# mLSTM cell and leaky-ReLU feed-forward: another order of rows for w_in and x, and values loaded by one request

## The chip, the cores and the metric

The kernel runs on one core of a Trainium2 chip. The metric is the time of one execution on the device in microseconds (us); lower is better. Engines are named as in the profile: PE is TensorE (PEld its weight loads), DVE is VectorE, ACT is ScalarE, POOL is GpSimd, SP is SyncE, whose queue (SPq) issues nearly all DMAs of this kernel.

## What is computed

An mLSTM cell over 4 batches, 8 heads, 768 tokens and head dimension 40 gives `y`, and a feed-forward block follows (3072 tokens, model width 320, inner width 2048). Inputs q, k, v, the gates i, f, o, and the weights `w_in` (320 x 2048) and `w_out` (2048 x 320), which come as 64-bit floats.

```python
for t in range(S):
    m_new = np.maximum(f[:, :, t] + m, i[:, :, t])
    f_stab, i_stab = np.exp(f[:, :, t] + m - m_new), np.exp(i[:, :, t] - m_new)
    m = m_new
    C = f_stab * C + i_stab * outer(v_t, k_t)
    n = f_stab * n + i_stab * k_t
    y[:, :, t] = sigmoid(o_t) * (C @ q_t) / np.maximum(np.abs(n @ q_t), 1.0)
x = y.transpose(0, 2, 1, 3).reshape(B * S, H * D)      # 3072 x 320
h = x @ w_in
out = np.maximum(0.01 * h, h) @ w_out
```

## The kernel before

**Steps.** Time is cut into 6 chunks of 128 tokens. A step `s` is one chunk of one batch, so there are 24 steps, `c, b = divmod(s, 4)`. Each chunk gives 512 tokens (4 batches x 128), one group of the feed-forward block. While group `c - 1` runs through the feed-forward block on TensorE, the cells of chunk `c` are computed between its pieces: `ff_units` makes a list of some 30 pieces per group, `cell_units` the list of cell parts, and the main loop (L1043 to L1103) calls a piece and then those cell parts whose place in a list written by hand (`place` for chunk 1, `pairs` later) has come. PE, DVE, ACT and POOL run in the order in which the program issues; so does SP's queue, where an instruction that waits holds up all behind it.

**Three kinds of steps.** Chunk 0 (steps 0 to 3) is written out in `first_chunk`. Steps 4 to 7 (chunk 1) use `u_parts` and `u_plain`. Steps 8 to 23 use `u_parts` and `u_mix`. `ahead(s)` prepares a step some pieces before it is needed: `prep_qs` (L487) or `prep_kq` (L505, L511), loads for step `s + 2`, `state_next` (L592, the old state times its decay, on POOL), `prep_vu` (L478, keys times gates, on POOL) and in some places `prep_mask` (L450, the mask added to the decay tile `w`, on POOL). `feed(s)` loads k (L356) and v (L359) and then `spread(s)` loads the decay rows into `w` (L413). `u_parts` multiplies scores (L614) and the new state (L619, which reads the values from the state tile `S` and the scaled keys of L478), then L624 and L596 on DVE.

**Values.** From chunk 1 on, the values of a step stand in the tile `S` (`S_v[n]`, n = s % 4) in two halves of tokens and two halves of 20 of the head dimension with a gap between. Four requests per step put them there directly from DRAM.

**x and w_in.** The feed-forward block needs x transposed, `xT`: the 320 features lie as 5 slots of 64 on 64 partitions, twice (on partitions 0 to 63 and 64 to 127), because two matmuls of 64 rows work side by side for two different columns of `w_in` (L759, `w_row`). The slots of the two halves stand in different orders (`SLOTS`), and a slot holds 64 neighbouring features. In chunks 0 and 1, `gate` (L650, L654) or `u_plain` (L676, L681) makes x with tokens on partitions, and `u_x` transposes it on PE (L742, L743) and copies it to `xT` by five copies on ACT (L745 to L749). From chunk 2 on, `u_mix` makes x transposed in blocks of 32 on DVE (L702, L706, L709 on POOL, L713), stores it to a DRAM tile `x_dr` by four requests (L716), and `gather_x` reads it back by four (L730) into `xT`, a tile with one buffer, after the last L759 of the group before.

**Weights.** `load_weights(n)` loads a slab of `w_in` by ten requests (L229) or one of `w_out` by one (L234); `narrow_weights` turns 64-bit floats into 32-bit ones on ACT (L247) and DVE (L249 to L263), in small pieces that the main loop issues between units of chunk 1.

**The end of a group.** `fast_units` multiplies by `w_out` in 14 products (L835) whose results are combined by DVE (L862, L887, L892), ACT and POOL (L868, L876, L882). The PSUM banks of `ph` and `po` are four, used in turn, so that the first L759 of the next group needs banks that L887 has read.

Of the kernel before, what the change touches and what calls it, by code (L numbers as in the profile page):

```python
# [9 lines left out]
F32 = mybir.dt.float32  # L10
# [8 lines left out]
def kernel(  # L19
# [26 lines left out]
    nc = tc.nc  # L46
# [19 lines left out]
    KF = Dm // P  # L66
    KR = Dm - KF * P
    KC = Dm // DP
    SLOTS = ([0, 2, 4, 1, 3], [1, 3, 0, 2, 4])
    assert NB * P == S and NF * P == FF and NF % 4 == 0 and D <= DP and H == 2 * PR and BH <= P  # L70
    assert KR == DP and KC == 5 and KC * DP == Dm and GT * 4 <= 2048

# [101 lines left out]
        at = (2 * slot + e) * P  # L174
        return w_in[DP * r : DP * (r + 1), n, at : at + P]

    def run_of(r, at):

        ks = SLOTS[r][at:]
        return ks[0], next((i for i in range(1, len(ks)) if ks[i] != ks[i - 1] + 2), len(ks))  # L180

    HW = 2 * Dm
    wide = moe_w_in.dtype == U64
    raws = {}
# [19 lines left out]
    def load_weights(n):  # L204

        m = n - QN
        if n < QN:
            dst = w_in[:, n, :]
        else:
            dst = w_out[:, 2 * m : 2 * m + 2, :].rearrange("p a d -> p (a d)")  # L210
        to = dst
        if wide:
            if n < 2:
                at = NF * GT - 2 * WC * (n + 1)
                raw = acts_l[:, at : at + 2 * WC].bitcast(U64)
            elif n < QN:
                raw = raw_t[:, WC * (n - 2) : WC * (n - 1)]
            elif m < 2:
                raw = w_out[:].rearrange("p f d -> p (f d)")[:, (2 + m) * WC : (3 + m) * WC].bitcast(U64)
            else:  # L220
                at = (4, 0, 1, 2, 3, 4)[m - 2] * HW
                raw = raw_t[:, at : at + HW]
            raws[n] = (raw, dst)
            to = raw
        if n < QN:
            src = moe_w_in[:, n * QC : (n + 1) * QC].rearrange("(k p) (r c) -> r p k c", p=DP, r=2)
            for slot in range(KC):
                for r in range(2):
                    nc.sync.dma_start(  # L229
                        to[DP * r : DP * (r + 1), 2 * P * slot : 2 * P * (slot + 1)], src[r, :, SLOTS[r][slot], :],  # L230
                    )
        else:
            rows = moe_w_out[2 * m * P : 2 * (m + 1) * P, :]
            nc.sync.dma_start(to.rearrange("p (a d) -> p a d", d=Dm), rows.rearrange("(a p) d -> p a d", p=P))  # L234
# [29 lines left out]


    a_dr = dr.tile([NB, 2, 2, BH, SL], F32, name="a_dr")
    x_dr = dr.tile([NS, Dm, P], F32, name="x_dr")
    gT, gL = {}, {}
    m0s = {}
    bus = {}  # L270
# [73 lines left out]
    def load(s):  # L344
        c, b = divmod(s, B)
        rows = ts(c, P)
        d = st.setdefault(s, {})
        n = s % NL
        d.update(k=kn[:, n], q=qn[:, n])
        if c == 0:  # L350
            d["va"] = S_t[n][:, 1]
            parts = [(d["k"][:, :, :D], k), (d["q"][:, :, :D], q), (d["va"][:, :, :D], v)]
            for dst, src in parts:
                nc.sync.dma_start(dst, src[b, :, rows, :].rearrange("h p d -> p h d"))
            return
        nc.sync.dma_start(d["k"][:, :, :D], k[b, :, rows, :].rearrange("h p d -> p h d"))  # L356
        for u in range(2):
            for i in range(2):
                nc.sync.dma_start(  # L359
                    S_v[n][ts(u, SL), u, :, i, :DB],  # L360
                    v[b, :, c * P + u * SL : c * P + (u + 1) * SL, DB * i : DB * (i + 1)].rearrange("h p d -> p h d"),
                )

    def load_o(s):
        c, b = divmod(s, B)
# [6 lines left out]
    def natural(s, i):  # L372

        t = rb_t[s % NR][:, i]
        return t[:, : H * D].rearrange("p (h d) -> p h d", d=D)
# [30 lines left out]
    def spread(s):  # L406

        c, b = divmod(s, B)
        d = st[s]
        w = wk.tile([P, H, P], F32, name="w", bufs=NL)  # L410
        d["w"] = w[:].rearrange("p h t -> p (h t)")[:, : H * SL].rearrange("p (h t) -> p h t", t=SL)
        for u in range(2):
            nc.sync.dma_start(d["w"][ts(u, SL)], a_dr[c, 0, u, b * H : (b + 1) * H, :].partition_broadcast(SL))  # L413

# [230 lines left out]
    def gate(s):  # L645

        d = st[s]
        d["x"] = wk.tile([P, Dm], F32, name="x")
        x3 = d["x"][:].rearrange("p (h d) -> p h d", d=D)
        nc.vector.scalar_tensor_tensor(  # L650
            x3, in0=d["o"].rearrange("p (h d) -> p h d", d=D), scalar=1.0, in1=d["pa"][:, :, :D],
            op0=ALU.add, op1=ALU.mult,
        )
        nc.gpsimd.tensor_tensor(x3, x3, d["den"][:].unsqueeze(2).to_broadcast([P, H, D]), op=ALU.mult)  # L654

    def u_plain(s):

        c, b = divmod(s, B)
        d = st[s]
        prep_o(s)  # L660
        hN = psc.tile([P, H, 2, V1], F32, name="hN", tag="c")
        m = mixed(s)
        for h in range(H):
            for u in range(2):
                nc.tensor.matmul(
                    hN[ts(u, SL), h].rearrange("p k d -> p (k d)"), lhsT=m[:, u, h, :], rhs=S_v[s % NL][:, u, h, :, :V1],
                    start=True, stop=True,
                )
        state_next(s, 1)
        den = wk.tile([P, H], F32, name="den")  # L670
        denominators(den[:], hN[:, :, 0, DB])
        if b < 2:
            d["x"] = wk.tile([P, Dm], F32, name="x")[:]
        else:
            d["x"] = wk.tile([P, H, D1], F32, name="hn")[:].rearrange("p h d -> p (h d)")[:, :Dm]
        nc.vector.scalar_tensor_tensor(  # L676
            d["x"].rearrange("p (n d) -> p n d", d=DB), in0=natural(s, 2).rearrange("p h (k d) -> p (h k) d", d=DB), scalar=1.0,
            in1=hN[:].rearrange("p h k d -> p (h k) d")[:, :, :DB], op0=ALU.add, op1=ALU.mult,
        )
        x3 = d["x"].rearrange("p (h d) -> p h d", d=D)  # L680
        nc.gpsimd.tensor_tensor(x3, x3, den[:].unsqueeze(2).to_broadcast([P, H, D]), op=ALU.mult)  # L681
        state_add(s, 1)

    def u_mix(s):
# [26 lines left out]
            state_add(s, 1)  # L711
        xq = wk.tile([P, PR * P], F32, name="x")
        nc.vector.transpose(in_blocks(xq[:]), xb[:].rearrange("p (j n) d -> p j n d", n=TB))  # L713
        to = x_dr[s].rearrange("(j n i) t -> n i j t", n=4, i=DB)
        for n in range(4):
            nc.sync.dma_start(to[n], xq[QW * n : QW * n + DB].rearrange("p (j t) -> p j t", t=P))  # L716
        del st[s]

    def gather_x(s):

        c, b = divmod(s, B)
        if ("xT", c) not in st:
            st["xT", c] = wk.tile([P, KC, GT], F32, name="xT", bufs=1)
        xT = st["xT", c]
        src = x_dr[s].rearrange("(k p) t -> p k t", p=DP)
        for r in range(2):
            at = 0
            while at < KC:
                k0, n = run_of(r, at)
                nc.sync.dma_start(xT[DP * r : DP * (r + 1), at : at + n, ts(b, P)], src[:, k0 : k0 + 2 * n - 1 : 2, :])  # L730
                at += n

    def u_x(s):

        c, b = divmod(s, B)
        d = st[s]
        if b == 0:
            st["xT", c] = wk.tile([P, KC, GT], F32, name="xT", bufs=1)
        xT = st["xT", c]
        xt = psc.tile([P, KF + 1, P], F32, name="xt", tag="c")  # L740
        for kk in range(KF):
            nc.tensor.transpose(xt[:, kk, :], d["x"][:, ts(kk, P)], ident[:])  # L742
        nc.tensor.transpose(xt[:KR, KF, :], d["x"][:, KF * P :], ident[:])  # L743
        tok = ts(b, P)
        nc.scalar.copy(xT[:, :KF, tok], xt[:, :KF, :])  # L745
        nc.scalar.copy(xT[:DP, KF + 1 :, tok], xt[DP:, :KF, :])
        nc.scalar.copy(xT[DP:, KF : 2 * KF, tok], xt[:DP, :KF, :])
        nc.scalar.copy(xT[:DP, KF, tok], xt[:DP, KF, :])
        nc.scalar.copy(xT[DP:, 2 * KF, tok], xt[:DP, KF, :])  # L749
        del st[s]  # L750


    def ff_units(g):
        xT = st["xT", g]

        def rows(j, ph, cols, slots):
            for slot in slots:
                for r in range(2):
                    nc.tensor.matmul(  # L759
                        ph[r][:, cols], lhsT=w_row(r, slot, j), rhs=xT[DP * r : DP * (r + 1), slot, cols],  # L760
                        start=(slot == 0), stop=(slot == KC - 1),
                    )

# [17 lines left out]

        def half(j, h):
            ph = [psf.tile([P, GT], F32, name=f"ph{r}", tag="mm") for r in range(2)]
            cols = ts(h, GT // 2)
            rows(j, ph, cols, range(KC))
            relu(j, ph, cols)

# [131 lines left out]
    def ahead(s):  # L919

        if s < NS:
# [9 lines left out]
            if s + NR < NS:  # L931
                load_late(s + NR, 0)
                load_late(s + NR, 1)
                if s + NR >= 2 * B:
                    spread_q(s + NR)
            state_next(s, 0)
            prep_vu(s)
            if s + 1 <= 2 * B:
                prep_mask(s + 1)
# [195 lines left out]
```

## Time and profile before

| | |
|---|---|
| time, median of 3 runs | 510.27 us (510.13 to 510.55) |
| span of the profiled execution, first to last instruction | 508.0 us |
| median less this span | 2.27 us |
| mean granted TensorE clock | 0.983 |
| requests of v in chunks 1 to 5 (L359) | 80 of 40 KB |
| stores of x (L716), gathers (L730) | 64 of 40 KB, 32 of 96 KB and 32 of 64 KB |
| DMA packets | 165290, of these under 512 B 128816 |
| DMA engines' share of the span, queue of SP | 52.2% |

The profiled execution has no time of its own beside its span; what lies around the span is taken as the difference to the median. Times inside the profile count from the first instruction. A line such as L759 is a line of the kernel before. Rows of groups give busy time and mean duration of one instruction, then the idle time of its engine just before. Matmul ends are modelled, and each f32 matmul appears as two records.

### The profile page before, as it was taken

The numbers are of one execution on the slowest core, as the hardware profiler recorded it, in microseconds if no ns is written. First come the engines' busy times: TensorE is split into PE (matmuls) and PEld (weight loads), VectorE is DVE, ScalarE is ACT, GpSimd is POOL, SyncE is SP. The second block draws the span as 40 slices with busy tenths as digits, with TensorE's granted clock in tenths as the row PEclk, the third lists the DMA queues.
The fourth block names the chain that finished last, engine by engine and source line by source line (L and its number), as shares of the span: only waits on it lengthen the run. The fifth ranks groups of instructions, "written<-read, shape, count | busy, mean of one in ns | idle before, by whom it ended". The sixth has DMA issues, their size and how long they took to land.

```text
span 508.0 us, 12526 instructions
## 1 busy us (share of the span) xinstructions
PE 492.0 (97%) x4981; PEld 366.6 (72%) x4981; DVE 308.1 (61%) x515; ACT 171.5 (34%) x478; POOL 137.7 (27%) x175
## 2 busy tenths in 40 slices
PE   8878999999999999999999999999899999999997
PEld 7766878767655489955589855599755599744797
DVE  4779898899954778635765826764825664101321
ACT  3664864652722510323411323311213411022210
POOL 4243443360402404413104614014612003000020
PEclk9877999999999999999999999999999999999999
DMA  9977687888765551565663566564466212200001
GB/s 116 146 204 154 149 219 185 168 152 175 155 145 87 131 124 46 133 130 144 147 132 92 115 137 170 137 141 97 109 135 177 68 53 62 69 1 1 1 1 52
DMA packets 165290, 59.21 MB, mean 117 GB/s; under 512 B 128816, under 2 KB 156016, under 8 KB 165232
## 3 DMA queue, kind: packets, MB, share of 16 engines
q1 hardware_dynamic: 164848, 58.28, 52.2%
q8 instruction: 39, 0.64, 0.5%
q14 instruction: 19, 0.16, 0.1%
q10 hardware_dynamic: 384, 0.13, 0.1%
HBM read 51.68 MB, written 6.70 MB: 115 GB/s over the span
## 4 chain that ended last, share of the span: by engine, by line
PE 79%; DVE 9%; DMA 3%; ACT 3%; POOL 2%; issue 2%; SPq 2%; ACTq 0%; POOLq 0%; DVEq 0%
PE ph L759 36%; PE po L835 26%; PE po L794 6%; PE pT L695 3%; PE sd L614 3%; SPq L359 1%; PE sd L619 1%; DMA S<-in_v_dram 1%; ACT kqT L540 1%; PE tkq L548 1%; DVE raw L261 1%; DMA rb<-in_q_dram 1%; DMA w<-a_dr 1%; PE pa L641 1%; DVE qn L511 1%
## 5 line engine op out<-in xcount | busy, mean ns | idle before, releaser
L759 PE MATMUL ph<-xT,w_in 64*128 64x512 f32 (+1 forms) x1120 | 216.2, 538 | 2.4 <-DVE y L887 1.4
L759 PEld LDWEIGHTS ph<-xT,w_in 64*128 64x128 f32 x1120 | 108.6, 189 | 95.1 <-issue 86.3
L767 ACT ACTIVATE acts<-ph 128x512 f32<-128x512 f32 (+1 forms) x112 | 53.9, 533 | 179.0 <-PE ph L759 178.9
L835 PEld LDWEIGHTS po<-w_out,acts 128*128 128x128 f32 x640 | 87.3, 190 | 3.8 <-issue 3.8
L835 PE MATMUL po<-w_out,acts 128*128 128x160 f32 x640 | 89.1, 300 | 0.0
L450 POOL TENSOR_TENSOR w<-w,i 128x512 f32<-128x512 f32 x20 | 26.9, 1345 | 117.3 <-DMA w<-a_dr 117.2
L624 DVE TENSOR_TENSOR qn<-w,sd 64x512 f32<-64x512 f32 x40 | 27.4, 684 | 40.2 <-PE sd L619 20.5
L458 ACT ACTIVATE w<-w,gT 128x64 f32<-128x64 f32 (+1 forms) x192 | 50.8, 348 | 2.7 <-POOL w L450 1.7
L592 POOL TENSOR_TENSOR S<-S,f 40x336 f32<-40x336 f32 x36 | 32.0, 889 | 67.3 <-PE pT L695 36.3
L835 PE MATMUL po<-raw,acts 128*128 128x160 f32 x320 | 45.5, 300 | 0.0
L835 PEld LDWEIGHTS po<-raw,acts 128*128 128x128 f32 x320 | 43.9, 190 | 0.3
L794 PE MATMUL po<-w_out,acts 128*128 128x320 f32 x128 | 36.5, 436 | 0.0
L702 DVE STREAM_TRANSPOSE hb<-pT 128x512 f32<-128x512 f32 x16 | 11.5, 717 | 31.0 <-PE pT L695 30.8
L794 PEld LDWEIGHTS po<-w_out,acts 128*128 128x128 f32 x128 | 23.6, 190 | 9.3 <-issue 0.3
L511 DVE TENSOR_TENSOR qn<-kqT,ea 64x512 f32<-64x512 f32 x32 | 28.4, 888 | 1.0
L709 POOL TENSOR_TENSOR xb<-xb,den 128x320 f32<-128x320 f32 x16 | 11.7, 729 | 56.8 <-DVE xb L706 56.6
L596 DVE TENSOR_TENSOR S<-S,sd 40x336 f32<-40x336 f32 x36 | 18.1, 503 | 12.1 <-POOL S L592 11.2
L614 PEld LDWEIGHTS sd<-kqT 40*64 40x64 f32 x640 | 19.9, 135 | 6.1 <-issue 6.1
L822 DVE TENSOR_TENSOR raw<-acts 128x1024 f32<-128x1024 f32 x10 | 11.8, 1222 | 18.3 <-ACT acts L767 18.2
L713 DVE STREAM_TRANSPOSE x<-xb 128x512 f32<-128x512 f32 x16 | 18.2, 1140 | 7.6 <-POOL xb L709 7.6
L835 PE MATMUL po<-raw 128*128 128x160 f32 x160 | 22.5, 299 | 0.0
L835 PEld LDWEIGHTS po<-raw 128*128 128x128 f32 x160 | 22.0, 190 | 0.0
(151 smaller groups left out, 551.8 us busy)
## 6 DMA issues: line engine op xcount, KB each, us to landing
w<-a_dr SPq DMA_DIRECT2D x40, 128.0 KB
rb<-in_k_dram SPq DMA_DIRECT2D x64, 80.0 KB
rb<-in_q_dram SPq DMA_DIRECT2D x64, 80.0 KB
rb<-in_o_gate_dram SPq DMA_DIRECT2D x64, 80.0 KB
ea<-a_dr SPq DMA_DIRECT2D x32, 128.0 KB
kn<-in_k_dram SPq DMA_DIRECT2D x24, 160.0 KB
raw<-in_moe_w_out_dram SPq DMA_DIRECT2D x6, 640.0 KB
S<-in_v_dram SPq DMA_DIRECT2D x80, 40.0 KB
```

The lines of the kernel that those rows point to most:

```text
L450: nc.gpsimd.tensor_tensor(w, w, cm2.unsqueeze(1).to_broadcast([P, H, SL]), op=ALU.add)
L458: yield nc.scalar.activation(w[:, h, :], w[:, h, :], AF.Exp, bias=gT[c][:, 0, bh : bh + 1], scale=1.0)
L511: nc.vector.tensor_tensor(mixed(s)[rows, 1 - r], d["kqT"][rows, 1].rearrange("p (h t) -> p h t", t=SL), d["ea"][rows], op=ALU.mult,)
L592: nc.gpsimd.tensor_tensor(new, old, g, op=ALU.mult)
L596: nc.vector.tensor_tensor(new, new, st[s]["dC", u], op=ALU.add)
L614: nc.tensor.matmul(bank[1 - u][toks, h, :], lhsT=kqT[rows, 0, ts(h, SL)], rhs=kqT[rows, 1, ts(h, SL)], start=True, stop=True,)
L624: nc.vector.tensor_tensor(mixed(s)[toks, u], w[toks], bank[1 - u][toks], op=ALU.mult)
L713: nc.vector.transpose(in_blocks(xq[:]), xb[:].rearrange("p (j n) d -> p j n d", n=TB))
L759: nc.tensor.matmul(ph[r][:, cols], lhsT=w_row(r, slot, j), rhs=xT[DP * r : DP * (r + 1), slot, cols], start=(slot == 0), stop=(slot == KC ...
L767: nc.scalar.activation(acts[:, f, cols], ph[r][:, cols], AF.Prelu, alpha=0.01)
L794: nc.tensor.matmul(po[n][:], lhsT=acts[:, f, ts(n, P)], rhs=w_out[:, f, :], start=(f == 0), stop=(f == NF - 1),)
L835: nc.tensor.matmul(bank[:], lhsT=left[:, f, :], rhs=right[:, f, :], start=f == 0, stop=f == KH - 1)
```

## The change

Feature `5 p + k` now stands on partition `p` in slot `k`, for both halves alike, in `w_in` and in `xT`. `u_mix` stores the whole 128-partition tile with its padding rows in one request; `gather_x` reads 64 partitions of 2560 contiguous bytes in one request for each half. `xT` is laid out by batch first, so that L759 reads it in runs of 128 columns. In chunks 0 and 1 x is written in the new order by the DVE instruction of `gate` and `u_plain`, multiplied in that order by POOL (`scale_x`), and `u_x` needs four copies in place of five. The values of a step from chunk 1 on are loaded by one request into an unused part of the tile `w` (which is now allocated in `load`), and `place_v`, called in `ahead` between `state_next` and `prep_vu`, copies them into `S` by two POOL instructions.

```diff
-    SLOTS = ([0, 2, 4, 1, 3], [1, 3, 0, 2, 4])
...
-            src = moe_w_in[:, n * QC : (n + 1) * QC].rearrange("(k p) (r c) -> r p k c", p=DP, r=2)
+            src = moe_w_in[:, n * QC : (n + 1) * QC].rearrange("(p k) (r c) -> r p k c", p=DP, r=2)
...
-                        to[DP * r : DP * (r + 1), 2 * P * slot : 2 * P * (slot + 1)], src[r, :, SLOTS[r][slot], :],
+                        to[DP * r : DP * (r + 1), 2 * P * slot : 2 * P * (slot + 1)], src[r, :, slot, :],
...
-        for u in range(2):
-            for i in range(2):
-                nc.sync.dma_start(
-                    S_v[n][ts(u, SL), u, :, i, :DB],
-                    v[b, :, c * P + u * SL : c * P + (u + 1) * SL, DB * i : DB * (i + 1)].rearrange("h p d -> p h d"),
-                )
+        w = wk.tile([P, H, P], F32, name="w", bufs=NL)
+        flat = w[:].rearrange("p h t -> p (h t)")
+        d["w"] = flat[:, : H * SL].rearrange("p (h t) -> p h t", t=SL)
+        d["vn"] = flat[:, H * SL : H * (SL + D)].rearrange("p (h d) -> p h d", d=D)
+        nc.sync.dma_start(d["vn"], v[b, :, rows, :].rearrange("h p d -> p h d"))
+
+    def place_v(s):
+        for u in range(2):
+            toks = ts(u, SL)
+            nc.gpsimd.tensor_copy(
+                S_v[s % NL][toks, u, :, :, :DB], st[s]["vn"][toks].rearrange("p h (k d) -> p h k d", d=DB),
+            )
...
+    def x_by(x, m):
+        return x[:].rearrange("p (k m a) -> p m a k", k=KC, m=m)
+
+    def scale_x(x, den):
+        x4 = x[:].rearrange("p (k h a) -> p k h a", k=KC, h=H)
+        by = den[:].unsqueeze(1).unsqueeze(3).to_broadcast([P, KC, H, DP // H])
+        nc.gpsimd.tensor_tensor(x4, x4, by, op=ALU.mult)
...
-            d["x"].rearrange("p (n d) -> p n d", d=DB), in0=natural(s, 2).rearrange("p h (k d) -> p (h k) d", d=DB), scalar=1.0,
-            in1=hN[:].rearrange("p h k d -> p (h k) d")[:, :, :DB], op0=ALU.add, op1=ALU.mult,
+            x_by(d["x"], 2 * H), in0=natural(s, 2).rearrange("p h (k a i) -> p (h k) a i", k=2, i=KC), scalar=1.0,
+            in1=hN[:].rearrange("p h k d -> p (h k) d")[:, :, :DB].rearrange("p n (a i) -> p n a i", i=KC),
+            op0=ALU.add, op1=ALU.mult,
...
-        to = x_dr[s].rearrange("(j n i) t -> n i j t", n=4, i=DB)
-        for n in range(4):
-            nc.sync.dma_start(to[n], xq[QW * n : QW * n + DB].rearrange("p (j t) -> p j t", t=P))
+        nc.sync.dma_start(x_dr[s].rearrange("(j p) t -> p j t", p=P), xq[:].rearrange("p (j t) -> p j t", t=P))
...
-        src = x_dr[s].rearrange("(k p) t -> p k t", p=DP)
+        src = x_dr[s].rearrange("(m w) t -> m w t", w=QW)[:, :DB, :].rearrange("m (a k) t -> m a (k t)", k=KC)
         for r in range(2):
-            at = 0
-            while at < KC:
-                k0, n = run_of(r, at)
-                nc.sync.dma_start(xT[DP * r : DP * (r + 1), at : at + n, ts(b, P)], src[:, k0 : k0 + 2 * n - 1 : 2, :])
-                at += n
+            nc.sync.dma_start(xT[DP * r : DP * (r + 1), b, :], src)
...
-        nc.scalar.copy(xT[:, :KF, tok], xt[:, :KF, :])
-        nc.scalar.copy(xT[:DP, KF + 1 :, tok], xt[DP:, :KF, :])
-        nc.scalar.copy(xT[DP:, KF : 2 * KF, tok], xt[:DP, :KF, :])
-        nc.scalar.copy(xT[:DP, KF, tok], xt[:DP, KF, :])
-        nc.scalar.copy(xT[DP:, 2 * KF, tok], xt[:DP, KF, :])
+        for r in range(2):
+            rows = ts(r, DP)
+            nc.scalar.copy(xT[rows, 0::2, :], xt[:DP])
+            nc.scalar.copy(xT[rows, 1::2, :], xt[DP:, :KF])
...
-                        ph[r][:, cols], lhsT=w_row(r, slot, j), rhs=xT[DP * r : DP * (r + 1), slot, cols],
+                        ph[r][:, cols], lhsT=w_row(r, slot, j), rhs=xT[DP * r : DP * (r + 1), slot, bs, :],
...
             state_next(s, 0)
+            place_v(s)
             prep_vu(s)
```

More of the change, by code (lines that the diff above doesn't have):

```diff
@@ L175, in w_row @@
         return w_in[DP * r : DP * (r + 1), n, at : at + P]
-    def run_of(r, at):
-        ks = SLOTS[r][at:]
-        return ks[0], next((i for i in range(1, len(ks)) if ks[i] != ks[i - 1] + 2), len(ks))
     HW = 2 * Dm
@@ L266 @@
     a_dr = dr.tile([NB, 2, 2, BH, SL], F32, name="a_dr")
-    x_dr = dr.tile([NS, Dm, P], F32, name="x_dr")
+    x_dr = dr.tile([NS, PR * P, P], F32, name="x_dr")
     gT, gL = {}, {}
@@ L409, in spread @@
         d = st[s]
-        w = wk.tile([P, H, P], F32, name="w", bufs=NL)
-        d["w"] = w[:].rearrange("p h t -> p (h t)")[:, : H * SL].rearrange("p (h t) -> p h t", t=SL)
         for u in range(2):
@@ L648, in gate @@
         d["x"] = wk.tile([P, Dm], F32, name="x")
-        x3 = d["x"][:].rearrange("p (h d) -> p h d", d=D)
         nc.vector.scalar_tensor_tensor(
-            x3, in0=d["o"].rearrange("p (h d) -> p h d", d=D), scalar=1.0, in1=d["pa"][:, :, :D],
-            op0=ALU.add, op1=ALU.mult,
-        )
-        nc.gpsimd.tensor_tensor(x3, x3, d["den"][:].unsqueeze(2).to_broadcast([P, H, D]), op=ALU.mult)
+            x_by(d["x"], H), in0=d["o"].rearrange("p (h a k) -> p h a k", h=H, k=KC), scalar=1.0,
+            in1=d["pa"][:, :, :D].rearrange("p h (a k) -> p h a k", k=KC), op0=ALU.add, op1=ALU.mult,
+        )
+        scale_x(d["x"], d["den"])
+    def x_by(x, m):
[4 more added lines that the diff above has]
+        nc.gpsimd.tensor_tensor(x4, x4, by, op=ALU.mult)
     def u_plain(s):
@@ L676, in u_plain @@
         nc.vector.scalar_tensor_tensor(
-            d["x"].rearrange("p (n d) -> p n d", d=DB), in0=natural(s, 2).rearrange("p h (k d) -> p (h k) d", d=DB), scalar=1.0,
-            in1=hN[:].rearrange("p h k d -> p (h k) d")[:, :, :DB], op0=ALU.add, op1=ALU.mult,
-        )
-        x3 = d["x"].rearrange("p (h d) -> p h d", d=D)
-        nc.gpsimd.tensor_tensor(x3, x3, den[:].unsqueeze(2).to_broadcast([P, H, D]), op=ALU.mult)
+            x_by(d["x"], 2 * H), in0=natural(s, 2).rearrange("p h (k a i) -> p (h k) a i", k=2, i=KC), scalar=1.0,
+            in1=hN[:].rearrange("p h k d -> p (h k) d")[:, :, :DB].rearrange("p n (a i) -> p n a i", i=KC),
+            op0=ALU.add, op1=ALU.mult,
+        )
+        scale_x(d["x"], den)
         state_add(s, 1)
@@ L722, in gather_x @@
         if ("xT", c) not in st:
-            st["xT", c] = wk.tile([P, KC, GT], F32, name="xT", bufs=1)
+            st["xT", c] = wk.tile([P, B, KC * P], F32, name="xT", bufs=1)
         xT = st["xT", c]
-        src = x_dr[s].rearrange("(k p) t -> p k t", p=DP)
+        src = x_dr[s].rearrange("(m w) t -> m w t", w=QW)[:, :DB, :].rearrange("m (a k) t -> m a (k t)", k=KC)
         for r in range(2):
-            at = 0
-            while at < KC:
-                k0, n = run_of(r, at)
-                nc.sync.dma_start(xT[DP * r : DP * (r + 1), at : at + n, ts(b, P)], src[:, k0 : k0 + 2 * n - 1 : 2, :])
-                at += n
+            nc.sync.dma_start(xT[DP * r : DP * (r + 1), b, :], src)
     def u_x(s):
@@ L737, in u_x @@
         if b == 0:
-            st["xT", c] = wk.tile([P, KC, GT], F32, name="xT", bufs=1)
-        xT = st["xT", c]
+            st["xT", c] = wk.tile([P, B, KC * P], F32, name="xT", bufs=1)
+        xT = st["xT", c][:, b, :].rearrange("p (k t) -> p k t", t=P)
         xt = psc.tile([P, KF + 1, P], F32, name="xt", tag="c")
@@ L743, in u_x @@
         nc.tensor.transpose(xt[:KR, KF, :], d["x"][:, KF * P :], ident[:])
-        tok = ts(b, P)
-        nc.scalar.copy(xT[:, :KF, tok], xt[:, :KF, :])
-        nc.scalar.copy(xT[:DP, KF + 1 :, tok], xt[DP:, :KF, :])
-        nc.scalar.copy(xT[DP:, KF : 2 * KF, tok], xt[:DP, :KF, :])
-        nc.scalar.copy(xT[:DP, KF, tok], xt[:DP, KF, :])
-        nc.scalar.copy(xT[DP:, 2 * KF, tok], xt[:DP, KF, :])
+        for r in range(2):
+            rows = ts(r, DP)
+            nc.scalar.copy(xT[rows, 0::2, :], xt[:DP])
+            nc.scalar.copy(xT[rows, 1::2, :], xt[DP:, :KF])
         del st[s]
     def ff_units(g):
-        xT = st["xT", g]
+        xT = st["xT", g][:].rearrange("p b (k t) -> p k b t", t=P)
         def rows(j, ph, cols, slots):
+            bs = slice(cols.start // P, cols.stop // P)
             for slot in slots:
@@ L783, in half @@
             ph = [psf.tile([P, GT], F32, name=f"ph{r}", tag="mm") for r in range(2)]
-            cols = ts(h, GT // 2)
+            cols = slice(h * GT // 2, (h + 1) * GT // 2)
             rows(j, ph, cols, range(KC))
```

## The prediction, made before the change was run

> **What bounds the kernel now.** I read the page first, then the stage windows, TensorE's waits, the chain of waits in order of time, and the timelines of GpSimd (POOL), VectorE (DVE) and the DMA queue (SPq).
>
> ```profile
> PE 492.0 (97%) x4981; PEld 366.6 (72%) x4981; DVE 308.1 (61%) x515; ACT 171.5 (34%) x478; POOL 137.7 (27%) x175
> ```
>
> TensorE lacks 16.0 us of the 508.0 us span. The four stretches from the first matmul of feed-forward group 1 to that of group 5 show where it does not lack any:
>
> ```profile
> 139.38:214.18 74.80, 74.80 (x777) 54.16 (x776) 49.27 (x76) 21.45 (x65) 21.27 (x25) 1.00 0.49 109
> 214.18:289.07 74.89, 74.89 (x776) 54.16 (x776) 46.08 (x81) 21.05 (x64) 24.07 (x26) 1.00 0.56 129
> 289.07:365.26 76.19, 74.79 (x775) 54.08 (x775) 46.48 (x78) 21.14 (x64) 23.56 (x26) 1.00 0.58 130
> ```
>
> Columns are the stretch, its length, then busy time of PE, PEld, DVE, ACT, POOL. Only the third has idle TensorE, 1.40 us. After 139 us nothing but that can be won, unless a matmul itself changes. TensorE's waits name it, and those before 139 us:
>
> ```profile
> PE ph L759 <- DVE y L887: 1.4, 1, 1.4
> PE tq L520 <- POOL y L487: 0.9, 1, 0.9
> PE tg L328 <- DVE hn L676: 0.7, 1, 0.7
> PE sd L619 <- POOL vu L478: 0.7, 1, 0.7
> ```
>
> The chain behind the first of these (start, length, what):
>
> ```profile
> 339.91 1.57 PE pT L695 x48
> 341.53 0.63 SPq L359
> 342.26 0.59 SPq L359
> 342.90 0.63 SPq L359
> 343.58 0.63 SPq L413
> 344.26 3.33 DMA w<-a_dr
> 347.74 1.24 POOL w L450
> 349.06 0.76 POOL S L592
> 349.90 0.74 POOL xb L709
> ```
>
> Value loads wait for pT, the decay load w queues behind them, and POOL sits in the mask addition L450 while the scaling L709 queues behind it; VectorE is then late up to L887. The last two waits, at 75.4 and 77.3 us, hang on this chain:
>
> ```profile
> 72.20 0.36 DVE x L676
> 72.69 0.73 POOL x L681
> 73.42 1.93 POOL y L487
> 75.42 0.91 POOL S L592
> 76.40 0.86 POOL vu L478
> 77.30 0.30 PE sd L619 x3
> ```
>
> **SP's queue.** Of 4 value requests 3 go, of 4 stores 3, of 4 gathers 2: 8 fewer per step in the chunked part. Issues back to back take 5.22 us per 8 (L730), 0.65 each, so 5.2 us per step and 21 us per 75-us chunk. In the third stretch the request for w at 343.58 stands behind two value groups (3 requests less each, 2 x 1.95 us), and the new value load no longer waits for pT (its target is a part of w's own buffer, last read at L624, long before). So w leaves at about 339.6, and L450 ends near 345 rather than 349. The 1.40 us stall goes: -1.4. In the second stretch the same sum moves L450 from 270.95 to about 267. All other SP relief lies beside a busy TensorE: 0. The early request of rb for step 4 comes 2 us sooner, but the 0.7 us that TensorE waits for it at 50.6 is covered, since ScalarE is in the xT copies until 51.5: 0.
>
> **POOL's copies.** place_v adds two 64x320 copies per step between L592 and L478, 40 in all. The trace has a COPY of 64x64 at 234 ns and memsets of 64x192 and 64x512 at 253 and 520, a slope of 0.83 ns an element: 234 + 256 x 0.83 = 0.45 us. From above: a two-input multiplication of 320 elements takes 0.72 undisturbed (L654). With gaps of 0.08 a pair costs 1.05 to 1.6 us; VectorE is full here, and L487 shows what that does (0.72 alone, 1.97 at 73.38). I take 1.4, nearer the upper end for that row. The copies wait for the value load, which stands ahead of w on SP, and w is awaited earlier by L450: no new wait. Queued behind them is L478, and for L478 TensorE waits.
> Step 4: L478 ends 56.2, needed at 59.97: hidden. Step 5: on the path, +1.4. Step 6: L478 ends 91.58, needed 92.50, so 0.5 is bare; but VectorE's L624 then waits for ScalarE until 94.77, 1.1 us after the scores, which covers it. Step 7: 1.8 us of slack cover it. In the chunks there are two pairs, 2.8 us, before the last L882, which in the second stretch ends 287.83, needed at 287.95. This is paid only because L450 frees POOL 4 us earlier; without that, about 2 us per chunk come back as stalls.
>
> **VectorE's outputs.** L650 and L676 (4 each) now write x with a step of 64 elements, 256 bytes. Three rows of the trace price this:
>
> ```profile
> L505 DVE STREAM_TRANSPOSE kqT<-rb 128x512 f32<-128x512 f32 x32 | 20.8, 687 | 0.3
> L713 DVE STREAM_TRANSPOSE x<-xb 128x512 f32<-128x512 f32 x16 | 18.2, 1140 | 7.6 <-POOL xb L709 7.6
> L702 DVE STREAM_TRANSPOSE hb<-pT 128x512 f32<-128x512 f32 x16 | 11.5, 717 | 31.0 <-PE pT L695 30.8
> ```
>
> L702 writes without gaps, L505 with a step of 2 elements (8 bytes), L713 with 4 (16 bytes): 0.42 us more for 512 elements, 0.26 for 320. Bounds 0 and 0.28 (against L505); a gain is excluded, since the write before was contiguous. I take 0.28. [...]
> On the path up to 77 us: VectorE works almost without a pause from 30.9 (L650 of step 1) to 51.8, then waits 1.19 at 52.98 for ScalarE, which itself follows step 3's x. Following the order of the queues, of three slow L650 about 0.4 pass this point; contention of VectorE with step 4's copies adds 0.3 (L253 on w_out takes 0.49 alone, 1.17 beside POOL); L676 of step 4 adds 0.28. Sum +1.0 in L487. The L328 wait at 105.7 is VectorE's again: L676 of step 6, +0.28. The second multiplication (L654, L681) keeps its 320 elements and only cuts them otherwise; L450, broadcast in the middle, has 2.5 ns an element, L709 2.3: below 0.1, taken as 0.
>
> **ScalarE.** Per step, five copies of 365, 370, 364, 260, 258 ns become two of 384 elements and two of 256. By the slope between 128 and 256 elements (0.86 ns) that is 2 x 480 + 2 x 367 = 1.69 us against 1.62, with one gap less: 0.
>
> **The matmuls of L759** read xT in runs of 128 with a step between them, 4 runs for 512 columns, 2 for 256. No row shows this form. L619 reads 42 columns in two runs, 214 ns; L614 64 in one, 220: no price. L665 (two runs) has 232, L695 (one) 224: at most 8 ns a run. I take 0. Loading w_in keeps its 20 requests of 1280 elements over two slabs' runs of equal length; only the distance of rows changes: 0, within 0.5.
>
> **The sum:** -1.4 + 1.4 + 1.0 + 0.28 = +1.3 us. Span 509.3. The median stands 2.27 us above the span (510.27 against 508.0), time that the profile does not show: 511.6.
>
> **Rivals.**
> - *The copies and writes cost their lower bounds* (copies 0.45, strided writes 0, no contention): -1.4 + 1.05 = -0.35, so 509.9. For it: TensorE has slack elsewhere. Against: L713. This is no measurable change.
> - *The queues fall apart at step 5.* L487 takes 1.97 at 73.38 only because it meets VectorE's L263 and L249. Started 0.5 to 1 us later it may miss one, and take 0.72: -1.25. With the lower bounds: 508.7, faster. It decides from a shift of L487 past 74.8, the end of L263, without L263 moving along; against it, L263 sits behind the same L676.
> - *The stall does not go, because POOL is later by the copies than it is earlier by w.* If w comes 2 us earlier rather than 4 and copies take 1.6, the last L882 of the third stretch moves from 364.1 by -2 + 3.2 to 365.3: the 1.4 us stay and a like stall of about 1 us comes at 289: 511.6 + 2.4 = 514.0. It decides once a pair of copies exceeds half of what w gains.
> - *A run costs TensorE 8 ns:* 800 x 3 x 8 + 320 x 8 = 21.8 us over two row groups working side by side, 10.9 us: 522. Against it: L619.
>
> [...]
>
> **How the numbers follow.** A measurement of this kernel tells 0.2%, 1.0 us, from no change. Forecast 0.4, lower bounds 0.2, queues falling apart 0.2, stall kept 0.15, runs 0.05. The forecast's own bounds (a pair of copies 1.05 to 1.6, strided writes 0 to 0.28 each, w_in 0.5 either way) spread it from 510.7 to 512.6, so about a quarter of its 0.4 lies below 511.3. Faster 0.2; same 0.2 + 0.1 = 0.3; slower 0.3 + 0.15 + 0.05 = 0.5. The range leaves out the runs and the tails of the two outer cases: 508.8 to 514.0.
>
> **What would show it.** Right: third stretch near 74.8; L450 idle before it less by 4 us; COPY rows of 0.45 to 0.8; L650 and L676 above 0.7; TensorE's wait for L478 at 2 us or more; group 1's first matmul near 142.1 rather than 139.4. Wrong: L759 above 593 ns, stretches still over 75, or L676 at 0.44.

## The result, and the profile after

The changed kernel takes 512.66 us (median of 7 runs, 511.57 to 514.68) against 510.27 us: a ratio of 1.0061, 95% interval 1.0034 to 1.0088. It is slower, as forecast (511.6 us, 508.8 to 514.0). By the medians that is 2.4 us. The profiled execution took 511.57 us, the shortest of the seven, and has a span of 509.8 us, so 1.8 us more than the one before. In the experiments below, the executions of a kernel with a mean granted clock of 0.973 or less take 1.4 to 4.2 us longer by median than its others; six of these seven of the change have so low a clock, and 25 of the 105 of the kernel before that were timed there. Line numbers move by about one: L760 is the old L759, L618 the old L619, L477 the old L478, L486 the old L487, L648 and L684 the old L650 and L676.

The first matmul of group 1 starts at 143.36 us instead of 139.38, so 3.98 us are lost before it. From there to the start of group 5 2.3 us are won (298.1 us instead of 300.4), to the end of the span 2.2. The stage windows of the changed kernel, one row from group to group as before:

```profile
143.36:218.06 74.70, 74.70 (x777) 54.06 (x776) 50.04 (x76) 21.45 (x65) 28.93 (x35) 1.00 0.60 135
218.06:292.75 74.69, 74.69 (x776) 54.05 (x776) 48.25 (x81) 20.92 (x64) 26.80 (x34) 1.00 0.61 138
292.75:367.44 74.69, 74.69 (x777) 54.05 (x776) 48.15 (x80) 20.92 (x64) 26.90 (x34) 1.00 0.63 142
```

Every stretch is now as long as TensorE's work. The third was 76.19. POOL (last busy column before the clock) has 3 to 8 us more per stretch, and it costs nothing there. The mask addition of step 21, the old L450 at 347.71, comes earlier in the third stretch. It ended 59.9 us after the start of the stretch (348.98 against 289.07) and now ends 46.9 us after it, by this row of POOL's timeline:

```profile
337.92 1.78 POOL L449 TENSOR_TENSOR w<-w,i 128x512 f32<-128x512 f32 x1 [11.86 <-DVE acts L854]
```

In the whole kernel POOL waited 117.2 us for `w` before its mask additions; now it waits 8.6.

TensorE's longest waits after the first 50 us, by the list of waits of the changed kernel (total, times, longest):

```profile
PE sd L618 <- POOL vu L477: 2.9, 2, 2.2
PE ph L760 <- ACT acts L768: 0.7, 1, 0.7
PE tq L519 <- POOL y L486: 0.7, 1, 0.7
PE hN L673 <- DVE S L595: 0.5, 1, 0.5
```

The 1.4 us wait for L887 is gone, and so is the one of L328 for VectorE. The wait for L768, at 55.7, was 0.3 in the kernel before. The wait for the key scaling, 0.7 us before, is now 2.2 at step 5 and 0.7 at step 6. POOL's timeline at step 5 (start, length, instruction, count) shows why:

```profile
72.25 1.97 POOL L486 TENSOR_TENSOR y<-rb,gT 128x320 f32<-128x320 f32 x1
74.31 0.89 POOL L591 TENSOR_TENSOR S<-S,f 40x336 f32<-40x336 f32 x1
75.26 1.59 POOL L361 COPY S<-w 64x320 f32<-64x320 f32 x2
76.93 0.72 POOL L477 TENSOR_TENSOR vu<-kn,gT 128x320 f32<-128x320 f32 x1
```

The two copies stand between the state and the key scaling, as they were issued. What follows on TensorE is the surprise. The window from 76 to 90 us, first before, then after; the three numbers at the end are granted clock, DMA share and GB/s:

```profile
76.00:90.00 14.00, 13.30 (x264) 11.75 (x260) 11.62 (x19) 7.30 (x17) 5.77 (x7) 1.00 0.83 185
```

```profile
76.00:90.00 14.00, 12.29 (x208) 10.53 (x212) 7.34 (x15) 4.07 (x11) 3.38 (x4) 0.76 0.88 221
```

And the 60 records of L759 (now L760) that follow step 5's scores, from TensorE's timeline of each kernel:

```profile
78.38 6.75 PE L759 MATMUL ph<-xT,w_in 64*128 64x256 f32 x60
```

```profile
79.41 8.82 PE L760 MATMUL ph<-xT,w_in 64*128 64x256 f32 x60
```

The same 60 records take 2.07 us longer at a granted clock of 0.76. They start only 1.03 us late and end 3.1 us late. The late start is small because this execution began the transposes of step 5 at 74.28, 1.12 us earlier than the one before (75.40). From there to the end of the 60 records it takes 13.95 us, the kernel before 9.73. Of these 4.2 us the longer wait makes 1.5; the other 2.7 are slower matmuls, 0.6 in the scores and 2.07 in the 60 records. The wait itself is the smaller part of the loss.

The rows that carried the forecast's prices, from the groups of the changed kernel (busy time, mean ns, idle before):

```profile
L760 PE MATMUL ph<-xT,w_in 64*128 64x512 f32 x800 | 176.3, 593 | 0.0
L361 POOL COPY S<-w 64x320 f32<-64x320 f32 x40 | 24.7, 616 | 1.9
L748 ACT COPY xT<-xt 64x384 f32<-64x384 f32 x16 | 7.5, 471 | 13.1 <-PE xt L745 12.9
L648 DVE SCALAR_TENSOR_TENSOR x<-acts,pa 128x320 f32<-128x320 f32 x4 | 2.8, 698 | 1.5 <-ACT acts L493 1.4
L684 DVE SCALAR_TENSOR_TENSOR x<-rb,hN 128x320 f32<-128x320 f32 x2 | 1.3, 669 | 0.0
```

### The profile page after: what moved, and what is told of

Same layout as the page of the kernel before. It is cut to its first block, busy times and chain, and to the rows that moved or that the text cites. A ratio compares the mean times of both kernels' runs of the same rounds, so it can differ in the third digit from the quotient of the medians.

```text
span 509.8 us, 12365 instructions
## 1 busy us (share of the span) xinstructions
PE 493.9 (97%) x4981; PEld 367.5 (72%) x4981; DVE 313.7 (62%) x515; ACT 172.3 (34%) x470; POOL 159.2 (31%) x215
## 4 chain that ended last, share of the span: by engine, by line
PE 78%; DVE 9%; SPq 6%; DMA 3%; ACT 1%; issue 1%; POOL 1%; DVEq 0%; POOLq 0%
PE ph L760 36%; PE po L836 30%; PE po L795 3%; PE pT L703 3%; SPq L223 3%; PE sd L613 3%; SPq L348 2%; DVE raw L255 1%; DVE w_in L251 1%; SPq L369 1%; PE sd L618 1%; DVE raw L253 1%; DVE qn L623 1%; DMA raw<-in_moe_w_in_dram 1%; DVE w_out L257 1%
## 5 line engine op out<-in xcount | busy, mean ns | idle before, releaser
L760 PE MATMUL ph<-xT,w_in 64*128 64x512 f32 (+1 forms) x1120 | 217.1, 541 | 0.7 <-ACT acts L768 0.7
L760 PEld LDWEIGHTS ph<-xT,w_in 64*128 64x128 f32 x1120 | 109.1, 192 | 94.1 <-issue 87.1
L768 ACT ACTIVATE acts<-ph 128x512 f32<-128x512 f32 (+1 forms) x112 | 53.9, 534 | 180.3 <-PE ph L760 180.2
L449 POOL TENSOR_TENSOR w<-w,i 128x512 f32<-128x512 f32 x20 | 30.2, 1518 | 20.5 <-DVE acts L854 11.9
L510 DVE TENSOR_TENSOR qn<-kqT,ea 64x512 f32<-64x512 f32 x32 | 29.9, 933 | 1.0
L361 POOL COPY S<-w 64x320 f32<-64x320 f32 x40 | 24.7, 616 | 1.9
L823 DVE TENSOR_TENSOR raw<-acts 128x1024 f32<-128x1024 f32 x10 | 13.7, 1411 | 18.3 <-ACT acts L768 18.2
L618 PE MATMUL sd<-S,vu 64*40 64x42 f32 x576 | 20.2, 219 | 2.9 <-POOL vu L477 2.9
L888 DVE TENSOR_TENSOR hn<-hn,po 128x160 f32<-128x160 f32 x10 | 3.2, 321 | 31.8 <-issue 14.2
```

The costliest lines, as they stand in the source:

```text
L361: nc.gpsimd.tensor_copy(S_v[s % NL][toks, u, :, :, :DB], st[s]["vn"][toks].rearrange("p h (k d) -> p h k d", d=DB),)
L449: nc.gpsimd.tensor_tensor(w, w, cm2.unsqueeze(1).to_broadcast([P, H, SL]), op=ALU.add)
L510: nc.vector.tensor_tensor(mixed(s)[rows, 1 - r], d["kqT"][rows, 1].rearrange("p (h t) -> p h t", t=SL), d["ea"][rows], op=ALU.mult,)
L618: nc.tensor.matmul(dC[u][:, h].rearrange("p k d -> p (k d)"), lhsT=d["ku"][toks, h], rhs=S_v[s % NL][toks, u, h, :, :V1], start=True, stop ...
L760: nc.tensor.matmul(ph[r][:, cols], lhsT=w_row(r, slot, j), rhs=xT[DP * r : DP * (r + 1), slot, bs, :], start=(slot == 0), stop=(slot == KC ...
L768: nc.scalar.activation(acts[:, f, cols], ph[r][:, cols], AF.Prelu, alpha=0.01)
```

## The experiments

Each kernel was timed against the kernel before on the same chip; a ratio is to that kernel, with its 95% interval. The runs of the kernel before had medians of 509.1 (beside e1 to e4, one chip), 510.2 (beside e5 to e8, another chip) and 509.8 us (beside e9 to e12, that chip again). Single profiles of one kernel differ by some 2 us at the start of step 5 and by up to 4.5 us at group 1 (e7 and e11), so a reading that rests on one profile is weaker than one from the times.

**e1, the change without the values.** Four value requests straight into S, no copies.

```diff
-        nc.sync.dma_start(d["vn"], v[b, :, rows, :].rearrange("h p d -> p h d"))
+        for u in range(2):
+            for i in range(2):
+                nc.sync.dma_start(S_v[n][ts(u, SL), u, :, i, :DB], ...)
...
-            place_v(s)
```

> The change without its part on the values: four value requests per step straight into S as before, no copies by GpSimd; w_in, x_dr, xT, the strided VectorE writes and four ScalarE copies as in the change. Theory A (the loss before group 1 comes from the copies that stand ahead of L478 on GpSimd, and the long TensorE wait there also lowers the granted clock): first matmul of group 1 at 139.5 to 140.7 us, granted clock 1.00 from 70 to 90 us, TensorE's wait for the key scaling 1.2 us or less; the fewer x requests alone already take most of the 1.4 us stall before group 4; time 0.5 to 1.5 us below the kernel before, if the stall goes. Rival B (the strided VectorE writes of x are the loss): group 1 at 142 us or later, time 1 to 3 us above the kernel before.

508.6 us, ratio 0.9968 (0.9944 to 0.9992): faster than before. Group 1 starts at 139.68, the clock from 76 to 90 us is 1.00, the wait for the key scaling is back at 0.7, and the third stretch is 74.74. So the part on x alone removes the stall, and the loss before group 1 belongs to the values. Rival B falls as the main cause.

**e2, the kernel before with the values alone.** The opposite half: one request, `place_v` ahead of `prep_vu`, x and w_in as before.

```diff
...
+            place_v(s)
             prep_vu(s)
```

> The kernel before with only the part on the values: one value request per step into the tile w and two GpSimd copies ahead of the key scaling. Theory A: TensorE waits 2 us or more for the key scaling at step 5, granted clock falls below 0.9 between 76 and 90 us, first matmul of group 1 at 142 to 143.5 us; the stretch from group 3 to group 4 at 74.7 to 75 us; time 1 to 2.5 us above the kernel before. Rival B: group 1 at 139.5 to 140.5 us, time within 1 us of the kernel before or below it.

513.16 us, ratio 1.0055 (1.0031 to 1.0079): 2.8 us above by ratio and 4.1 by median, more than expected. Its profile, of the longest of the 12 executions, has the same wait and the same clock as the full change:

```profile
PE sd L624 <- POOL vu L483: 2.6, 2, 2.2
```

```profile
76.00:90.00 14.00, 10.92 (x154) 9.46 (x156) 9.25 (x14) 4.51 (x13) 5.20 (x6) 0.76 0.88 217
```

Group 1 starts at 145.39, later than expected, and its stretches are 74.70, 74.69 and 74.70. So the values alone also remove the 1.4 us stall (either half relieves SP enough), and they alone make the kernel slow.

**e3, the copies issued a step early.** For steps 5 to 8 the copies go behind the key scaling of the step before; all else as in the change.

```diff
-            place_v(s)
+            if s == B or s > 2 * B:
+                place_v(s)
             prep_vu(s)
             if s + 1 <= 2 * B:
                 prep_mask(s + 1)
+                place_v(s + 1)
```

> The change with the copies of steps 5 to 8 issued one step earlier, at the end of ahead(s) for step s + 1, behind the key scaling of step s instead of ahead of that of step s + 1; all else as in the change. Theory A: TensorE's waits for the key scaling fall to 0.9 us or less each, granted clock 1.00 from 70 to 90 us, group 1 at 140 to 141 us, the stretches after it stay at 74.7 and 74.0; time 2 to 3.5 us below the change, that is 0.5 to 1.5 us below the kernel before. Rival B: group 1 stays at 142 us or later and the time stays with the change, within 0.7 us.

508.24 us, ratio 0.9978 (0.9950 to 1.0007). The same 40 copies, placed elsewhere: the longest wait for the key scaling is 0.7, the clock 1.00, group 1 at 140.31, and the stretches after it are the change's. It lies 3.75 us below e4 on the same chip (2 to 3.5 expected); its interval includes 1, so this run alone does not show it below the kernel before (e10 below does). What it still waits for is the query scaling, 1.5 us at step 5, where the kernel before waits 0.9.

**e4, the change again.**

> The change itself once more, on the same chip as the others and beside the same runs of the kernel before. Both theories: 1.5 to 4 us above the kernel before. Theory A: the profile again shows a TensorE wait of about 2 us for the key scaling at step 5 and a granted clock below 0.9 between 76 and 90 us, with group 1 at 142 to 143.6 us. If the clock did not fall in this profile but the wait is there, group 1 would stand near 141 us.

511.99 us, ratio 1.0039 (1.0012 to 1.0066); wait 2.2, clock 0.76, 60 records in 8.97 us, group 1 at 143.55, all as expected.

**e5, the wait filled.** Ten dummy matmuls on TensorE in the place of the wait.

```diff
             split_qs(s)
+            if s == B + 1:
+                warm(10)
```

> The change with ten dummy matmuls of 128 columns (about 2.1 us at full clock) put on TensorE at step 5 between the transposes of q and the scores, where the change leaves it waiting 2.2 us for the key scaling. Theory A (the wait lets the granted clock fall, and the low clock costs as much again): wait for the key scaling at step 5 below 0.5 us, granted clock 0.95 or more from 76 to 90 us, the 60 records of ph after step 5 in 6.7 us instead of 8.8, group 1 at 140.3 to 141.5 us, time 1.5 to 3 us below the change. Rival C (the waits alone make the 4 us, the low clock costs nothing of its own): group 1 stays at 143 to 143.8 us, time as the change.

510.58 us, ratio 1.0011 (0.9987 to 1.0034). The ten matmuls take 2.50 us (the 2.1 of the forecast was my estimate). The wait at step 5 is gone and the clock stays at 1.00, although POOL needs as long as in the change, 5.4 us from the start of the query scaling to the end of the key scaling:

```profile
76.00:90.00 14.00, 14.00 (x280) 12.57 (x282) 9.82 (x18) 5.29 (x14) 5.44 (x7) 1.00 0.86 221
```

The 60 records are back at 6.75 us. Group 1 came to 142.31, later than I had expected, because this execution entered step 5 late: its transposes of q start at 75.89 (in the change at 74.28), after a wait of 1.55 for the query scaling. From there to group 1 it takes 66.4 us, the change 69.1: 2.7 us won by work that does nothing but keep TensorE busy, as much as the slower matmuls of step 5 had cost. Rival C, that the waits alone make the loss, falls. The times point the same way, 1.4 to 2.5 us less by ratio than the change (1.0039 and 1.0061, e4 on another chip), but the intervals of e5 and e4 overlap. Two of the 12 executions have a mean clock of 0.973 or less; of the change, in the first runs and in e4, 13 of 19.

**e6, the kernel before with POOL made late at step 5.**

```diff
+                for _ in range(4 if s == B + 1 else 0):
+                    nc.gpsimd.memset(d["vu"][:], 0.0)
                 nc.gpsimd.tensor_tensor(d["ku"], ...)
```

> The kernel before with four GpSimd memsets of 336 elements (about 1.5 us together) ahead of the key scaling, at step 5 alone; nothing of the change. Theory A: TensorE waits 1.8 to 2.5 us for the key scaling, granted clock below 0.9 between 76 and 90 us, the 60 records of ph after step 5 in 8 us or more, group 1 at 142 to 143.5 us, time 2.5 to 4 us above the kernel before. Rival C (a wait costs its own length): group 1 at 140.5 to 141.2 us, clock 1.00, time 1 to 1.8 us above.

513.69 us, ratio 1.0068 (1.0037 to 1.0099), so some 3.5 us. The four memsets took 2.03 us and not 1.5, and the wait grew by 1.84 to 2.54; rival C, at that length, has about 1.8 us. The clock from 76 to 90 us is 0.88, the 60 records take 8.43 us, and group 1 starts at 142.04, 2.7 us later than in the kernel before although this execution entered step 5 0.9 us earlier. Eight of the 12 executions have a mean clock of 0.973 or less. So a loss of this kind can be made in the old kernel, without any part of the change, by a late POOL at one step.

**e7 and e11, VectorE's writes without steps.** e3, with x of chunks 0 and 1 in the old order of features; the kernel leaves out the new order there, so its output is not that of the others.

```diff
-        return x[:].rearrange("p (k m a) -> p m a k", k=KC, m=m)
+        return x[:].rearrange("p (m a k) -> p m a k", k=KC, m=m)
```

> The change with the copies issued a step early (as in e3), and with VectorE writing x of chunks 0 and 1 without steps, in the old order of features; so the features of these chunks do not match the rows of w_in, and only the time is read. If the strided writes cost what the prediction summed (1.28 us before group 1): VectorE rows back at 475 and 436 ns and group 1 at 138.8 to 139.3 us, where e3 has 140.3. If other waits cover them: rows the same, group 1 at 139.8 to 140.3 us, time within 0.6 us of e3.

> e7 once more (x of chunks 0 and 1 in the old order of features, so only the time is read). Its first profile had the granted clock at 0.88 from 76 to 90 us without a wait of 2 us. If that was that execution alone: clock 1.00 now and group 1 at 139 to 140.3 us. If it belongs to this kernel: 0.9 or less again.

508.14 us, ratio 0.9967 (0.9936 to 0.9997), and in the second run (e11) 507.39 us, ratio 0.9953 (0.9924 to 0.9982). VectorE's rows are back at 472 and 436 ns. The first profile has group 1 at 142.35, outside both forecasts: waits of 1.3 and 0.7 us at step 5, another of 1.1 us later, and the clock at 0.88. The second has 0.5 and 0.7, clock 1.00, and group 1 at 137.89, earlier than forecast. Neither profile alone prices the writes.

**e8 and e9, GpSimd writes the new order.** e3, where VectorE multiplies in place in the gate tile and the multiplication by the denominators, on POOL, writes x with the step.

```diff
...
-        nc.gpsimd.tensor_tensor(x4, x4, by, op=ALU.mult)
+        nc.gpsimd.tensor_tensor(x_by(x, H), o.rearrange("p (h a k) -> p h a k", h=H, k=KC), by, op=ALU.mult)
```

> e3 with the new order of x written by GpSimd instead of VectorE: VectorE multiplies in place in the gate tile without steps, GpSimd's multiplication by the denominators writes with the step. Theory A: VectorE rows at 0.44 to 0.48 us, GpSimd's multiplication 0.75 to 1.3 us; group 1 within 0.7 us of e3's 140.3 either way, time 507.5 to 509. If a strided write costs GpSimd more than it cost VectorE, group 1 is later than in e3, because the multiplication stands ahead of the query scaling for which TensorE waits.

> e8 once more (copies early, VectorE multiplies in place without steps, GpSimd writes the new order), beside e3, e7 and the kernel before on one chip. If the strided VectorE writes cost time (theory D): 1 to 2 us below e3 and at most 0.7 us from e7; 0.3 to 0.7% below the kernel before. If the difference of e8 to e3 came from the chips (theory E): within 0.7 us of e3.

506.53 us, ratio 0.9959 (0.9925 to 0.9994), and 506.63 us, ratio 0.9943 (0.9913 to 0.9972). Both forecasts of e8 were missed: the time is below 507.5, and group 1 starts at 138.29, 2.0 us earlier than in e3 (139.27 in e9). POOL's multiplications take 975 ns (chunk 0), 775 and 760 with the step, and 941, 725 and 722 in the kernel before without it, so the order costs 0.03 to 0.05 us there, and VectorE is back at 474 and 436.

**e10, e3 again beside them.**

> e3 once more, on one chip with e7 and e8. Theory D: 0.5 to 2 us above e7 and e8. Theory E: within 0.7 us of both; in either case 0 to 0.4% below the kernel before, group 1 near 140.3 us if the granted clock stays at 1.00 from 76 to 90 us.

508.28 us, ratio 0.9966 (0.9941 to 0.9991): 1.65 us above e9 and 0.9 above e11. Theory E, that the difference came from the chips, falls. The sign is theory D's, that the strided writes cost time; but the intervals of the ratios overlap, and the medians overstate the size. The executions of these kernels lie in two groups. Of e7's twelve, six lie at 506.2 to 506.6 us with a mean granted clock of 0.979 or more and six at 509.7 to 511.0 us with 0.973 or less, so its median stands in the gap between them. e8, which also writes on VectorE without steps, has seven and five, and for that reason its median is 1.6 us lower than e7's. Among the executions above 0.973 alone, the medians beside each other are 507.5 (e10), 506.7 (e11) and 506.6 us (e9): 0.8 to 0.9 us go with the strided writes. The rest of the 1.65 is that four of e10's executions, and two of e9's, have the low clock; twelve executions do not show whether the writes do that too. The profiles do not settle it either. The wait for the query scaling at step 5, where the forecast put the loss, is 1.6 in e10 and 0.4 in e9:

```profile
PE tq L519 <- POOL y L486: 1.6, 1, 1.6
```

```profile
PE tq L519 <- POOL y L486: 0.4, 1, 0.4
```

But e7, without strided writes, waited 1.3 there, and the change, with them, 0.7.

In e10's profile this wait and 0.7 us behind it were also followed by a clock of 0.88 from 76 to 90 us, with 7.45 us for the 60 records and group 1 at 141.93. So the same kernel, after waits of nearly the same length, has a clock of 1.00 there in one profile (e3) and 0.88 in another.

**e12, the kernel before with the values alone, copies early.**

> The kernel before with the part on the values alone and its copies of steps 5 to 8 issued a step early; w_in, x and its requests as before. Theory A (place of the copies is what makes the part on the values slow): group 1 at 139.3 to 140.5 us, clock 1.00 from 76 to 90 us, stretches of 74.7, time 1 to 2.5 us below the kernel before; that is 4 us below e2. If the copies are dear wherever they stand: group 1 at 142 us or later, time above the kernel before.

507.55 us, ratio 0.9932 (0.9903 to 0.9962); clock 1.00, group 1 at 138.99 (slightly earlier than expected), stretches of 74.70, 74.69 and 74.70. It differs from e2 only in where the copies of four steps stand, and it is on the other side of the kernel before. By ratio it is level with e9, by median 0.9 us above it; both beat the kernel before, and by ratio the change too.

## Why the prediction was right, and where it was not

- **The sign and the main mechanism** were right: requests moved off SP end the stall, and the copies on POOL ahead of L478 at step 5 cost more than that. e1, e2, e3 and e12 show it from four sides. Two terms of the sum were not: the price of the wait, and the strided writes.
- **The stall (-1.4).** It went, and the stretches from group 1 to group 5 lost 0.10, 0.20, 1.50 and 0.51 us, 2.3 in all (74.53 to 74.02 is the last). The forecast had only the idle time of TensorE. It left out that the matmuls behind the stall were slower: the first 31 records of group 4 took 7.59 us, and 32 take 7.07 without a stall. The mask addition of step 21 came 13 us earlier in the stretch, not 4. Either half of the relief was enough (e1, e2).
- **The copies (+1.4).** 616 ns each by the mean, between the bounds of 450 and 720, but with a median of 452 and single ones up to 1594, so that most copies go at the lower bound and some far above the upper. The pair at step 5 took 1.59. The wait at step 5 grew from 0.7 to 2.2, as summed.
- **The mis-sized term** is what this wait costs. The sum took a wait at its own length, 1.4 us; at step 5 it went with 4.2. The granted clock was 0.76 from 76 to 90 us where the kernel before had 1.00, and the matmuls behind the wait took 2.7 us longer, which e5 took away; in e6, which has nothing of the change, the 60 records alone took 1.7 us longer. Step 6 was called covered; a wait of 0.7 us showed there.
- **The strided writes (+1.28 in the sum).** 698 and 668 ns instead of 475 and 436: 0.22 and 0.23 each, where the three transposes had given 0.28. The rows came near (the sign asked for, above 0.7, was just missed), but in the change the sum's +1.0 did not show: the query scaling L486 started at 72.25 (72.31 in e4), 1.1 us earlier than before and not 1.0 later, and the wait for it was 0.7 instead of 0.9. e10 beside e9 and e11 supports 0.8 to 0.9 us of the 1.28 in executions with the higher clock. The added 0.28 in the L328 wait at 105.7 did not come: TensorE arrived over 3 us later and no longer waited.
- **At nothing:** L760 keeps 593 ns, so runs of 128 columns cost nothing here, and that rival is out; ScalarE's copies take 471 and 368 ns, 1.68 us a step (forecast 1.69); the early value request and the copies cost nothing in the stretches from group 1 on.
- **The rivals.** L486 at step 5 took 1.97 or 1.98 us in every profile, so the queues did not fall apart in the way that would have made it faster. The stall kept at the group ends did not come either: POOL's last result of the third stretch was in time, since TensorE waited for nothing there.
- **The total** came near (1.8 us in the spans and 2.4 in the medians, 1.3 forecast) partly by luck, because misses have opposite signs: 4.0 instead of 2.7 before group 1, made up of a dearer wait and writes that did not show, and 2.2 instead of 1.4 won from there to the end of the span.
- **The forecast's own bounds** do not give 510.7 to 512.6. Added as they stand (a pair of copies -0.35 to +0.2, strided writes -0.96 to 0, w_in 0.5 either way) they spread 511.6 from 509.8 to 512.3, so, spread evenly, more than half of that case lay below 511.3, and "slower" was given too high a chance. The stated range covers both.

## What to carry to other kernels

When a request is replaced by a copy, look at what is queued behind the copy on its engine in the order of issue, not at how busy that engine is: the same 40 copies made this kernel slower in one place and faster a step earlier. Price a wait of TensorE by its length and by the records after it: read the granted clock of the window that follows. If a new order has to be written, price the strided write on each engine that could do it: here it took 0.22 us more on VectorE and 0.03 to 0.05 on GpSimd.

## What the runs showed of the hardware

- **The clock.** Idle times of TensorE of 0.7 and 2.2 us within 5 us (the change), or 0.9 and 2.5 (e6), were followed by a granted clock of 0.76 and 0.88 over the window from 76 to 90 us, and by 8.8 and 8.4 us for 60 records that take 6.75 in the kernel before. There, waits of 0.9 and 0.7 left it at 1.00. Waits of 1.5 and 0.7 left it at 1.00 in e3, and 1.55 and 0.69 in e10, the same kernel, were followed by 0.88. No run shows what decides between the two.
- **Strided writes.** A VectorE write with a step of 256 bytes took 0.22 to 0.23 us longer for 320 elements (698 against 475 ns, 668 against 436), a little less than the 0.28 estimated from the transposes L713 (16-byte step, 1140 ns for 512 elements) and L505 (8-byte step, 687). On GpSimd the same step took 0.03 to 0.05 us longer (975 against 941, 760 against 722, 775 against 725).
